# Batch 2's k loads later, each batch's second k turn earlier, and one pair of score groups in other PSUM banks

## The chip, the cores and the metric

The kernel runs on one core of a Trainium2 chip. The metric is the device time of one execution in microseconds (us). Three timed runs of the kernel before gave 306.77, 304.9 and 306.38, median 306.38 us; lower is better. The profile is of one more execution.

## The reference

For each of 8 batches and 8 heads of width 64, 576 queries attend to the last 64 positions (a causal sliding window); the result, as 4608 rows of 512 values, goes through two matrix products with a gate between.

```
scores = q @ k.T / sqrt(64)                    # 8 batches, 8 heads, 576 x 576
mask   = (i - j >= 0) & (i - j < 64)
attn   = softmax(where(mask, scores, -1e9))
x      = attn @ v  -> rows (batch, position), columns (head, d): 4608 x 512
h      = x @ w_in                              # 512 -> 2048
out    = (h * cos(h)) @ w_out                  # 2048 -> 512, float32
```

Inputs and outputs are float32; the kernel multiplies in bf16.

## The kernel before, in words

**Two streams.** The second part (the products with w_in and w_out) goes through the 4608 rows in nine tiles of 512 rows. For a tile, PE (TensorE) forms 16 blocks of h (L443), ScalarE takes a sine of each (L589), VectorE multiplies (L592), and PE multiplies by w_out (L604, 64 matmuls for a tile). The attention of a batch is cut into units of 64 queries by 128 keys (two heads of a pair, one query block), and units into groups of three or four. While tile t is in its second product, batch t + 1 goes through its softmax, group by group:

- scores on PE into a PSUM bank (`blocks_64`, L305), several groups by one call of `g_scores_across`;
- on VectorE the mask and the row maximum, one instruction a unit (`g_max`, L329); when it has run, the bank is free;
- the exponential on ScalarE, one a unit (`g_exp`, L340), its reciprocal sum on VectorE (`g_inv`, L347);
- the normalized weights w (`g_norm`, L354), for nearly all groups on GpSimd (POOL), for batch 1's first three on VectorE;
- the turn of w: for the groups in DIRECT by PE into a slot of the pool `ps_t` (`tw_ps`, L363) and a copy by VectorE (`g_put`, L117); for the others by a DMA transpose on SyncE's queue (`wT`, L366);
- the values on PE (`values`, L381), which read v, and the cast of their result (`put_x`, L117).

**Banks.** PSUM has eight. Five have names (O0, O1, X0, X1, S); a tile of the same name waits until the last one was read. The other three are the slots of `ps_t`, given out in turn: to the transposes `tw_ps`, the values `o_ps`, and in later batches to some scores. Batch 1's groups, counted from 0 here, get their scores in pairs: 0 and 1 in X1 and S, 2 and 3 in X0 and X1, 4 and 5 in S and X0, 6 and 7 in X1 and S, 8 and 9 in X0 and X1, 10 and 11 in S and X0. Groups 0 to 5, 8 and 9 of batch 1 are turned by PE, 6, 7, 10 and 11 by DMA.

**q, k and v.** From batch 2 on, q and k are loaded in five chunks each by GpSimd's DMA queue (`load_chunk`, L165), with the cast to bf16, and turned by a DMA transpose on SyncE's queue (`turn`, L250): q by one, k by two, the first for chunks 0 and 1, the second for chunks 2 to 4. The first part of a batch's scores reads the first turn of k, the second part both. v is loaded by GpSimd's queue (`load_v`, L171); its half blocks are copied to other partitions, for batch 1 by two DMAs on SyncE's queue (`spread_v`, L180), later by VectorE.

**What sets the order.** The program writes each engine's order itself. `at(time, step)` puts a step in a plan, `pump(time)` emits the steps that are due, and the main loop calls it between matmuls; the times are in steps of the plan, 32 to a tile, and not in us. Nothing is reordered after that: an instruction that waits holds up all behind it on its engine, and a DMA that waits holds up all behind it on its queue. Two kinds of rows keep q, k and v of two batches, so that loads for batch b + 1 run beside batch b.

Of the kernel before, what the change touches and what calls it, by code (L numbers as in the profile page):

```python
# [40 lines left out]
T = 2 * Q  # L41
# [23 lines left out]
def kernel(  # L65
# [44 lines left out]
    S_BANKS = ("X1", "S", "X0")  # L110
# [356 lines left out]
    def at(time, fn, *args):  # L467
        plan.append((time, len(plan), fn, args))
# [9 lines left out]
    n = n_first  # L478
    for t in range(B - 1):
        last = max(i for i, units in enumerate(groups) if units[0][0] == t + 1)  # L480
        time = T * t + Q - 1.4
        for i in range(last + 1 - n):
            time += PACE * len(groups[n - 1]) if i else 0
            if t and i == 4:
                time = max(time, T * t + Q + 4.3)
            if t == 0 and i % 2 == 0:
                at(time, g_scores_across, n, 2, (S_BANKS + S_BANKS)[i % 3:])
            elif t and i in (0, 4):
                at(time, g_scores_across, n, last + 1 - n if i else 4, "t t t S X1 X0".split() if i else "t t t X1".split())
            lags = LAGS[:2] + tuple(T * t + T - 0.65 - time + 0.01 * s for s in range(3)) if n == last and t else LAGS  # L490
            if t == 0 and i in (8, 9):
                lags = LAGS[:2] + ((2.2, 2.25) if i == 8 else (2, 2.05)) + LAGS[-1:]
            for lag, fn in zip(lags, (g_max, g_exp, g_inv, g_norm)):
                at(time + lag, fn, n, *("d" for _ in range(1) if fn is g_norm and n < n_first + 3))
            lag = (6.3 if t else 5.5 if i == 3 else 4.6) if n in direct else lags[-1]
            at(time + lag, g_trans, n)
            if n in direct:
                at(time + lag + 0.3, g_put, n)
            ready.update({unit: time + (lag + 1.3 if n in direct else 8.5) for unit in groups[n]})
            n += 1  # L500

    for b in range(1, B):
        t0 = T * (b - 1)
        if b > 1:
            for i, name in enumerate(("q", "k")):
                for c in range(NC):
                    time = 4 + 0.5 * (c + NC * i) if b == 2 else t0 - T + 8 + 0.9 * (c + NC * i)
                    if i and c > (3 if b == 2 else 1):
                        time = 26.9 if b == 2 else t0 - T + 22.5 + 1.5 * (c - 2)
                    at(time, load_chunk, name, b, c)  # L510
                for c, (lo, hi) in enumerate(((0, 2), (2, NC)) if i else ((0, NC),)):
                    at(t0 + 2.5 if c else t0 - (5.8 if b > 2 else 3.4) + 0.1 * i, turn, name, b, lo, hi)
            for c in range(5):
                at(t0 + 3.5 + 0.9 * c, load_v, b, c)
            for time, part in ((13.5, 0), (19.9, 2), (21.7, 3)):
                at(t0 + time, spread_v, b, part, None)
# [5 lines left out]
    for mt in range(1, n_mt):  # L522
        for p in range(PAIRS):
            time = max(ready[b, p - p % 2 + i // TU, j] for i in range(2 * TU) for b, j in (divmod(mt * TU + i % TU, NU),))
            time = max(time, 25.5) if mt == 1 else T * mt - (8.01 if mt == n_mt - 1 else 1.01)
# [118 lines left out]
```

## Time and profile before

| | before |
|---|---|
| timed runs, us | 306.77, 304.9, 306.38 |
| median, us | 306.38 |
| the profiled execution's own time, us | 305.0 |
| its span, us | 302.9 |
| PE busy, us | 286.5 |
| VectorE (DVE), ScalarE (ACT), GpSimd (POOL) busy, us | 221.4, 235.0, 172.2 |
| GpSimd's DMA queue (q0), SyncE's (q1), share of 16 DMA engines | 79.3%, 47.3% |
| HBM read and written, MB | 36.70, 9.44 |

The span goes from the first to the last instruction of the program; 2.1 us of the execution's own time lie around it. A row of the timeline is: start in us, length in us, engine, line, operation, output<-input, shape, count, and in brackets how long the engine had been idle and what ended that. SPq is SyncE's queue; its length is that of issuing, not of the transfer. A row of stretches is: from:to, length, then busy us and count of PE, PEld (weight loads), DVE, ACT, POOL, the granted clock, the share of the 16 DMA engines (several packets of one may overlap, so it can pass 1) and GB/s. A row of waits is: who <- for whom: us in all, times, the longest. A row of DMA issues is: output<-input, queue, count, KB each, us from issue to landing. A row of a DMA queue is: packets, MB, share of the engines. A row of the chain is: start, us, what. A row of one tile's instructions is: line, engine, operation, count, then the shortest, median and longest in ns, and the first and last start in us.

### The profile page before, as it was taken

To read this page: it belongs to the slowest core of one execution; us is meant where nothing else is said; L and a number is where in the kernel's file an instruction comes from. 1 tells how busy PE (TensorE), PEld (TensorE's weight loads), DVE (VectorE), ACT (ScalarE), POOL (GpSimd) and SP (SyncE) were. 2 spreads that over 40 slices of the span, in tenths; PEclk is the share of its full clock that TensorE was granted. 3 is DMA by queue.
4 is the path that set the end of the run, shared out by engine and by line. 5 is a ranking of instruction groups with operands and counts; after the bars stand their busy time and mean duration, and the time that the engine had idled before them with its cause. 6 is when DMAs were issued, how large, how long until landed. Compare 5 with 4: busy or idle time off the path is not lost.

```text
span 302.9 us, 8058 instructions
## 1 busy us (share of the span) xinstructions
PE 286.5 (95%) x2726; PEld 148.4 (49%) x2762; DVE 221.4 (73%) x852; ACT 235.0 (78%) x783; POOL 172.2 (57%) x204
## 2 busy tenths in 40 slices
PE   3789997999999999999999999989999999999996
PEld 2568743544454445444544454444544454454443
DVE  3899897778967897789678967896789778236701
ACT  5897898678997799879987998799869996116600
POOL 8997369792799368945995599549803620000000
PEclk9999999999999999999999999999999999999999
DMA  8999999999999999999999999999993470012011
GB/s 171 172 197 210 207 163 164 115 145 142 220 164 144 177 181 173 131 184 195 93 159 151 232 154 162 141 220 161 171 198 119 89 176 16 3 69 72 0 69 69
DMA packets 164841, 43.75 MB, mean 144 GB/s; under 512 B 153920, under 2 KB 160064, under 8 KB 164800
## 3 DMA queue, kind: packets, MB, share of 16 engines
q0 software_dynamic: 99360, 18.06, 79.3%
q1 hardware_dynamic: 65296, 24.98, 47.3%
q8 instruction: 21, 0.34, 0.5%
q14 instruction: 20, 0.16, 0.2%
q10 hardware_dynamic: 144, 0.20, 0.2%
HBM read 36.70 MB, written 9.44 MB: 152 GB/s over the span
## 4 chain that ended last, share of the span: by engine, by line
PE 67%; DMA 15%; POOL 6%; DVE 6%; issue 4%; ACT 0%; SPq 0%; POOLq 0%; DVEq 0%
PE h_ps L443 31%; PE out_ps L604 28%; DMA v<-in_v_dram 5%; DMA kX<-k 4%; POOL w L354 4%; DMA k<-in_k_dram 3%; DMA v<-v 3%; PE o_ps L381 2%; DVE s L329 2%; PE s_ps L305 2%; PE out_ps L455 1%; POOL v L171 1%; DMA q<-in_q_dram 1%; DVE negm L325 1%; PE tw_ps L363 1%
## 5 line engine op out<-in xcount | busy, mean ns | idle before, releaser
L604 PE MATMUL out_ps<-w_out,gT 128*128 128x512 bf16 x542 | 124.0, 379 | 1.7 <-issue 1.3
L443 PE MATMUL h_ps<-xT,w_in 128*128 128x512 bf16 x497 | 111.0, 379 | 1.1 <-issue 0.2
L354 POOL TENSOR_TENSOR w<-e,rden 128x512 bf16<-128x512 f32 (+1 forms) x75 | 73.0, 984 | 59.9 <-DVE rden L347 56.3
L592 DVE TENSOR_TENSOR gT<-h_ps,sin 128x512 bf16<-128x512 f32 x128 | 84.9, 688 | 30.2 <-ACT sin L589 30.2
L340 ACT ACTIVATE e<-s,negm 128x128 f32<-128x128 f32 x256 | 99.2, 403 | 1.9 <-DVE negm L329 1.8
L589 ACT ACTIVATE sin<-h_ps 128x512 f32<-128x512 f32 x128 | 73.7, 599 | 28.6 <-PE h_ps L443 28.1
L604 PEld LDWEIGHTS <-gT 128*128 128x128 bf16 x560 | 52.7, 98 | 60.5 <-issue 0.4
L443 PEld LDWEIGHTS <-w_in 128*128 128x128 bf16 x512 | 49.9, 98 | 59.1
L329 DVE CUSTOM_DVE_ANT_0 s<-s_ps,mask 128x128 f32<-128x128 f32 x256 | 57.9, 283 | 1.9 <-PE s_ps L305 1.7
L340 ACT ACTIVATION_READ_ACCUMULATOR e<-s,negm 128x1 f32 x256 | 51.9, 203 | 0.0
L171 POOL DMA_DIRECT2D v<-in_v_dram x40 | 34.1, 870 | 6.6 <-DMA w_out<-in_moe_w_out_dram 4.2
L117 ACT COPY out_sb<-out_ps 128x512 f32<-128x512 f32 (+1 forms) x18 | 10.5, 582 | 24.9 <-PE out_ps L604 19.3
L165 POOL DMA_DIRECT2D k<-in_k_dram x30 | 26.4, 893 | 1.7 <-DMA v<-in_v_dram 1.6
L165 POOL DMA_DIRECT2D q<-in_q_dram x30 | 25.4, 886 | 3.1 <-DMA w_out<-in_moe_w_out_dram 3.1
L117 DVE CAST xT<-o_ps 128x512 bf16<-128x512 f32 x28 | 18.3, 679 | 9.6 <-PE o_ps L381 9.3
L117 DVE COPY out_sb<-out_ps 128x512 f32<-128x512 f32 x18 | 12.3, 681 | 14.9 <-PE out_ps L604 14.9
L329 DVE DVE_READ_ACCUMULATOR2_ANT negm<- 128x1 f32 x256 | 20.9, 82 | 0.0
L347 DVE RECIPROCAL rden<-den 128x4 f32<-128x4 f32 (+1 forms) x80 | 13.5, 171 | 9.6 <-ACT e L340 7.7
L420 PE MATMUL h_ps<-xT,w_in 128*128 128x256 bf16 x128 | 15.5, 273 | 0.0
L420 PEld LDWEIGHTS <-w_in 128*128 128x128 bf16 x128 | 12.0, 98 | 1.4
L117 DVE COPY v<-v 64x1024 bf16<-64x1024 bf16 (+1 forms) x19 | 11.4, 601 | 0.4
L426 ACT ACTIVATE sin<-h_ps 128x512 f32<-128x512 f32 x16 | 9.1, 597 | 2.9 <-PE h_ps L420 2.9
(60 smaller groups left out, 187.5 us busy)
## 6 DMA issues: line engine op xcount, KB each, us to landing
out_dram<-out_sb SPq DMA_DIRECT2D x16, 512.0 KB, 7.7
v<-in_v_dram POOLq DMA_DIRECT2D x32, 128.0 KB, 6.2
q<-in_q_dram POOLq DMA_DIRECT2D x24, 128.0 KB, 8.7
k<-in_k_dram POOLq DMA_DIRECT2D x24, 128.0 KB, 7.9
w_in<-in_moe_w_in_dram POOLq DMA_DIRECT2D x2, 768.0 KB, 11.1
w_out<-in_moe_w_out_dram POOLq DMA_DIRECT2D x1, 1024.0 KB, 12.9
w_out<-in_moe_w_out_dram POOLq DMA_DIRECT2D x2, 512.0 KB, 15.5
wT<-w SPq DMA_TRANSPOSE x58, 5.0
```

The source lines that it names most:

```text
L117: {"a": nc.scalar.copy, "p": nc.gpsimd.tensor_copy}.get(engine, nc.vector.tensor_copy)(out, in_)
L165: nc.gpsimd.dma_start(out=st[name, b][:n, c].rearrange("p (h d) -> p h d", h=H), in_=src.rearrange("h p d -> p h d"))
L171: nc.gpsimd.dma_start(out=vt.rearrange("p (h d) -> p h d", h=H), in_=v[b, :, c * 128:c * 128 + n, :].rearrange("h p d -> p h d"))
L329: nc.vector.tensor_tensor_reduce(out=s[:, u], in0=s_ps[:, u], in1=mask[:, 2 - j % 2 if j else 0], scale=-scale if b else -1.0, scalar=BIG, ...
L340: nc.scalar.activation(e[:, u], s[:, u], AF.Exp, bias=negm[:, u:u + 1], scale=1.0 if n < n_first else -1.0, accum_out=den[:, u:u + 1])
L347: nc.vector.reciprocal(out=rden[:, 0:len(groups[n])], in_=den[:, 0:len(groups[n])])
L354: (nc.gpsimd if engine == "p" else nc.vector).tensor_tensor(out=w[:, 0:u], in0=e[:, 0:u], op=ALU.mult, in1=rden[:, 0:u].unsqueeze(2).to_br ...
L420: nc.tensor.matmul(out=st["h0", i][:, e], lhsT=w_in_sb[:, ks, ff * 128:ff * 128 + 128], rhs=st["xT", 0][:, ks, half], start=ks + e == 0, s ...
L443: nc.tensor.matmul(out=st["h", ff], lhsT=w_in_sb[:, ks, ff * 128:ff * 128 + 128], rhs=st["xT", mt][:, ks], start=start, stop=stop)
L589: nc.scalar.activation(sin, h_ps, AF.Sin, bias=math.pi / 2.0)
L592: nc.vector.tensor_tensor(out=gt[:, e], in0=h_ps, in1=sin, op=ALU.mult)
L604: nc.tensor.matmul(out=o_ps[e], lhsT=gT[ff // 2][:, ff % 2, ms * 128:ms * 128 + 128], rhs=w_out_sb[:, ff], start=ff == 0, stop=ff == n_ff - 1)
```

## The change

Three edits, all to the plan; every instruction of before is still there, once.

1. Batch 1's groups 8 and 9: scores in bank X0 and in the next slot of `ps_t`, where they had X0 and X1.
2. Batch 2's five k loads: at 27.1 to 27.5 of the plan. Before, four of them were at 6.5 to 8.0 and the last at 26.9. In GpSimd's order the four go from ahead of the w of group 3 to behind the w of group 9, the fifth from ahead of the w of group 9 to behind it, ahead of the w of groups 10 and 11. The order of the DMAs among themselves stays. Other batches' loads stay.
3. The second turn of k, for batches 2 to 7: right behind the first. In SyncE's order it moves ahead of two turns of w for batch 2, of four for batches 3, 4 and 6, and of three for batches 5 and 7 (there one turn of w stays between the two of k). Before, it was behind those and ahead of the stores of the tile.

The orders of PE, VectorE and ScalarE are the same, but for the bank.

```diff
             if t == 0 and i % 2 == 0:
-                at(time, g_scores_across, n, 2, (S_BANKS + S_BANKS)[i % 3:])
+                at(time, g_scores_across, n, 2, ("X0", "t") if i == 8 else (S_BANKS + S_BANKS)[i % 3:])
...
             for i, name in enumerate(("q", "k")):
                 for c in range(NC):
                     time = 4 + 0.5 * (c + NC * i) if b == 2 else t0 - T + 8 + 0.9 * (c + NC * i)
-                    if i and c > (3 if b == 2 else 1):
-                        time = 26.9 if b == 2 else t0 - T + 22.5 + 1.5 * (c - 2)
+                    if i and (b == 2 or c > 1):
+                        time = 27.1 + 0.1 * c if b == 2 else t0 - T + 22.5 + 1.5 * (c - 2)
                     at(time, load_chunk, name, b, c)
                 for c, (lo, hi) in enumerate(((0, 2), (2, NC)) if i else ((0, NC),)):
-                    at(t0 + 2.5 if c else t0 - (5.8 if b > 2 else 3.4) + 0.1 * i, turn, name, b, lo, hi)
+                    at(t0 - (5.8 if b > 2 else 3.4) + 0.1 * i + 0.1 * c, turn, name, b, lo, hi)
```

## The prediction

> **What bounds the kernel now.** I read the page first: one line for the span, one for TensorE.
>
> ```profile
> span 302.9 us, 8058 instructions
> PE 286.5 (95%) x2726; PEld 148.4 (49%) x2762; DVE 221.4 (73%) x852; ACT 235.0 (78%) x783; POOL 172.2 (57%) x204
> ```
>
> TensorE is the bound; all its idle time is 302.9 - 286.5 = 16.4 us. A change that takes no matmul away can win only idle time of PE in the stages that it touches, so next I read the busy time by stage and the list of PE's waits.
>
> ```profile
> 40.00:54.00 14.00, 11.93 (x146) 6.00 (x142) 11.51 (x76) 12.53 (x63) 11.86 (x15) 1.00 2.25 158
> ```
>
> ```profile
> PE tw_ps L363 <- POOL w L354: 1.5, 3, 0.9
> PE s_ps L305 <- DMA kX<-k: 0.6, 1, 0.6
> PE o_ps L381 <- DMA v<-v: 0.4, 1, 0.4
> ```
>
> From 40 to 54 us, while batch 1's softmax runs beside tile 0's second product, PE (the first pair of the row) loses 14.0 - 11.9 = 2.1 us. The first and the third of the waits shown lie there: transposes waiting for GpSimd's normalized weights w, and tile 1's first values waiting for the copy of v. The second, for a turned k, lies at 202 us. These are what the change can win: at most 2.1 + 0.6 = 2.7 us. The timeline of that stage, PE and then POOL:
>
> ```profile
> 46.73 0.24 PE L305 MATMUL s_ps<-kT,qT 64*64 64x128 bf16 x2
> 47.16 0.36 PE L305 MATMUL s_ps<-kT,qT 64*64 64x128 bf16 x10 [0.18 <-DVE negm L329]
> 47.44 1.04 PE L604 MATMUL out_ps<-w_out,gT 128*128 128x512 bf16 x4
> 49.34 0.34 PE L363 MATMUL tw_ps<-ident,w 128*128 128x128 bf16 x3 [0.86 <-POOL w L354]
> 50.12 0.34 PE L363 MATMUL tw_ps<-ident,w 128*128 128x128 bf16 x3 [0.45 <-POOL w L354]
> 50.30 1.03 PE L604 MATMUL out_ps<-w_out,gT 128*128 128x512 bf16 x3
> 51.16 0.33 PE L363 MATMUL tw_ps<-ident,w 128*128 128x128 bf16 x3
> ...
> 52.63 0.28 PE L381 MATMUL o_ps<-wT,v 128*64 128x64 bf16 x6
> 53.36 0.60 PE L381 MATMUL o_ps<-wT,v 128*64 128x64 bf16 x26 [0.44 <-DMA v<-v]
> 54.12 1.67 PE L604 MATMUL out_ps<-w_out,gT 128*128 128x512 bf16 x7 [0.16 <-issue]
> ```
>
> ```profile
> 44.86 3.54 POOL L165 DMA_DIRECT2D k<-in_k_dram  x4
> 48.46 2.39 POOL L354 TENSOR_TENSOR w<-e,rden 128x384 bf16<-128x384 f32 x3
> ...
> 54.67 0.83 POOL L354 TENSOR_TENSOR w<-e,rden 128x384 bf16<-128x384 f32 x1 [0.20 <-DVE rden L347]
> ```
>
> POOL issues batch 2's k loads for 3.54 us, and the three w behind them (groups 3, 4, 5) start with no wait of their own at 48.46: they were ready, and stood in line. PE stands still for the first two. The row at 54.67 is group 9's w. On VectorE:
>
> ```profile
> 46.32 0.17 DVE L347 RECIPROCAL rden<-den 128x3 f32<-128x3 f32 x1
> ...
> 47.28 0.17 DVE L347 RECIPROCAL rden<-den 128x3 f32<-128x3 f32 x1
> ...
> 48.46 0.29 DVE L329 CUSTOM_DVE_ANT_0 s<-s_ps,mask 128x128 f32<-128x128 f32 x1
> ...
> 50.50 0.36 DVE L117 COPY wT<-tw_ps 128x384 bf16<-128x384 bf16 x1 [0.43 <-PE tw_ps L363]
> 50.77 0.17 DVE L347 RECIPROCAL rden<-den 128x3 f32<-128x3 f32 x1
> ...
> 51.25 0.29 DVE L329 CUSTOM_DVE_ANT_0 s<-s_ps,mask 128x128 f32<-128x128 f32 x1
> ```
>
> The two first rows are groups 3's and 4's reciprocals, 48.46 is the last piece of group 8's maximum, 50.50 the copy of group 4's transposed weights, 50.77 group 6's reciprocal, and 51.25 the last piece of group 9's maximum. VectorE keeps that order in the changed kernel.
>
> **The change, part by part.**
>
> *Batch 2's k loads behind group 9's w.* POOL is free at 44.9 instead of 48.4. Group 3's w then starts when its reciprocal is done, 46.32 + 0.17 = 46.5, and takes 2.39 / 3 = 0.80: ready at 47.3. Group 4's: 47.28 + 0.17 = 47.45, ready at 48.3.
>
> *Group 9's scores in a slot of the transposes.* Groups 8 and 9 take twelve matmuls, of which the third waits for bank X1, which VectorE is still reading for group 6 (the released row at 47.16). From start to start the pair takes 47.44 - 46.73 = 0.71, its last ten 47.44 - 47.16 = 0.28, so without the wait some 0.28 x 12 / 10 = 0.34: 0.37 is won, since group 9's slot was last used three transposes ago. It has a price: the three slots go round, and now group 5's transposes get the slot of group 9's scores (before, that of group 2's transposes). They wait until VectorE has taken group 9's maximum, which stands in its queue behind the copies of groups 3 and 4 and group 6's reciprocal.
>
> The walk on PE: output product at 47.07; four matmuls (51.16 - 50.30 = 0.86) to group 3's transposes at 47.9, w is there; group 4's at 48.36 (0.06 after its w, as now: 48.46 + 2 x 0.80 = 50.06 and 50.12); 51.16 - 50.12 = 1.04 to group 5's, which PE reaches at 49.4. VectorE ends group 8's maximum at 48.46 + 0.29 = 48.75, the copy of group 3 takes 50.77 - 50.50 = 0.27, and from the copy of group 4 to the end of group 9's maximum it is 51.25 + 0.29 - 50.50 = 1.04: 50.06. Group 5's transposes start at 50.15, after a new wait of 0.75, yet 1.0 before their present 51.16. From there to the values it is 52.63 - 51.16 = 1.47: 51.62 instead of 52.63. If v's copy has landed, 0.1 for the first six and 54.12 - 53.36 = 0.76 for the rest bring the output product to 52.48 instead of 54.12: **1.65 us won.** With bank X1 kept, group 4's w at 48.3 sets the pace all the same, group 5's transposes would start at 49.5 and the values at 51.0; so the slot costs 0.6 here.
>
> *Does v's copy land in time?* It must land by 51.6; now it lands just before 53.36, where PE's wait ends.
>
> ```profile
> v<-v SPq DMA_DIRECT2D x1, 256.0 KB, 7.8
> q<-in_q_dram POOLq DMA_DIRECT2D x1, 64.0 KB, 5.8
> q0 software_dynamic: 2547, 0.32, 130.0%
> q1 hardware_dynamic: 442, 0.43, 53.4%
> q1 hardware_dynamic: 1678, 0.43, 114.0%
> ```
>
> The rows of q0 and the first of q1 are the stretch 46.6 to 50.6: GpSimd's queue (the last q and the k loads) moved 2,547 small packets while SyncE's moved the 0.43 MB of v's copy, in 4 us. The last row is 58 to 60: SyncE's queue alone moved 0.43 MB in 2 us. The last q load, issued some 0.7 before k's first at 44.86, lands 5.8 later at 50.0; with k gone nothing of POOL's queue comes after it. The bounds for the copy's landing are thus about 50.0 and, if k's packets never mattered, 53.3. I take the early end: that both queues moved at once, and that one alone is twice as fast, says that k's packets cost the copy time. [...]
>
> *k comes later: who waits?* Five loads of k, four of which were out by 48.4, now go behind group 9's w. That one ends at 54.67 + 0.83 = 55.5 now; its reciprocal stands on VectorE behind the first values, which come some 1.0 earlier or more, so I take 54.5. Five issues of 3.54 / 4 = 0.89 follow, to 58.9, ahead of the w of groups 10 and 11 and the v and q loads, which all come up to 2 us later.
>
> ```profile
> k<-in_k_dram POOLq DMA_DIRECT2D x1, 128.0 KB, 8.6
> k<-in_k_dram POOLq DMA_DIRECT2D x1, 64.0 KB, 4.0
> q<-in_q_dram POOLq DMA_DIRECT2D x2, 128.0 KB, 11.5
> kX<-k SPq DMA_TRANSPOSE x1, 6.6
> kX<-k SPq DMA_TRANSPOSE x1, 11.8
> 72.33 0.64 PE L305 MATMUL s_ps<-kX,qX 64*64 64x128 bf16 x32
> 78.19 0.75 PE L305 MATMUL s_ps<-kX,qX 64*64 64x128 bf16 x40
> ```
>
> A k load takes 4.0 us in light traffic and 8.6 in the present heavy one; batch 2's two turns took 6.6 and 11.8. First turn: its second chunk is issued at 55.4, so it lands between 55.4 + 4.0 + 6.6 = 66.0 and 55.4 + 8.6 + 6.6 = 70.6, and is wanted at 72.33 - 1.65 = 70.7. Second turn: last chunk issued at 58.0, landing between 58.0 + 4.0 + 6.6 = 68.6 and 58.0 + 8.6 + 11.8 = 78.4, wanted at 78.19 - 1.65 = 76.5. I take no wait: v and q loads that made the present one slow now come after it. The weights' turns of groups 10 and 11 stand behind both on SyncE, up to 11.8 us later than now, and are wanted by tile 2's values, which PE reaches only after the whole of the second product that these scores interrupt.
>
> *The second turn right behind the first, batches 3 to 7.* SyncE's weights' turns (one to four a batch) go behind it.
>
> ```profile
> 190.57 11.46 DMA kX<-k
> 211.66 1.04 PE o_ps L381 x59
> ```
>
> Batch 6's second turn is issued at 190.57 behind four weights' turns, lands at 202.03, and PE waits 0.6. Moved ahead of them it is issued some 6 us earlier: **0.6 us won.** The four go behind it, by about 5 us; the values that read them start at 211.66, and they have 8 us or more. The other batches' second turns do not hold PE now and come earlier; costed at nothing.
>
> *Sum:* 1.65 + 0.6 = 2.25. The profiled execution took 305.0, its span 302.9; the timed ones run from 304.9 to 306.77 with median 306.38. I set the sum against the middle of profiled run and median, 305.7: **303.4 us**.
>
> **The rivals.**
>
> *v's copy is no earlier.* Then the values start at 53.36 as now and all that was won before is given back there; only the 0.6 stays: 305.1. For it: no row shows the copy alone. Against it: the rates above.
>
> *The slot costs nothing.* If VectorE reaches group 9's maximum early enough, the 0.75 is not waited: 303.4 - 0.6 = 302.7, bounded by the copy's landing at 51.0. Against it: the order on VectorE is fixed and has copies of groups 3 and 4 ahead.
>
> *Slower: batch 2's second turn is late.* Its scores want it at 76.5, and every us past that is a us of PE: at the upper bound of 78.4 it costs 1.9, which leaves 305.3, and from 76.5 + 2.25 = 78.8 on the kernel is slower than before. If the last chunk of k took the 11.5 us that two q loads took at 64 to 66 us, the turn would land at 58.0 + 11.5 + 11.8 = 81.3, and the time would be 303.4 + 4.8 = 308.2. For it: k now travels beside q's turn and moves towards that heavy stretch. Against it: even with a turn of 11.8 us the last chunk may take 6.7 us, and the later traffic that made it 11.8 (v and q for the next batches) now comes behind it.
>
> Whether the issues themselves come late, now that they stand beside VectorE's copies and casts, this row bears on:
>
> ```profile
> L165 POOL DMA_DIRECT2D k<-in_k_dram x30: 733/939/974, 44.9 to 209.5; - x30
> ```
>
> Over all 30 issues the longest took 0.97 against a median of 0.94, beside a VectorE that is busy 73%: no issue here was held up. [...] By the row I give that no more than 0.05 of the chance below.
>
> **How the numbers follow.** Forecast (2.25 won, give or take half a us) 0.56; copy no earlier 0.20; slot free 0.10; second turn late 0.14, of which 0.07 ends slower than before. The likeliest case alone spans 302.4 to 304.6, since single runs differ by up to 1.9. The range of 301.8 to 306.2 takes in the first three and the mild part of the fourth. A measurement of this kernel can tell about 1%, 3 us, from no change; the forecast is 0.75%, so most of it counts as the same: faster by over 1% 0.18 (the free slot and the lucky half of the forecast), within 1% 0.75, slower 0.07.
>
> **What would show it.** PE's waits for GpSimd's w fall from 1.5 to about half of it; a new wait of about 0.75 appears at a transpose near 50 us, released by VectorE's maximum; the wait for v's copy is gone, and the copy's 7.8 us become 6 or less; the first s_ps from kX starts near 70.7; PE's wait for kX is gone. Wrong would be: the values again released by the copy at 53, a wait for kX at 71 or 77, or stage 40 to 54 as long as before with the wait merely under another name.

## The result and the profile after

| | before | after |
|---|---|---|
| median of the timed runs, us | 306.38 (5 runs, 304.9 to 307.09) | 302.33 (5 runs, 302.15 to 303.44) |
| ratio after / before, 95% interval | | 0.9899 [0.9866, 0.9932] |
| the profiled execution's own time, us | 305.0 | 302.33 |
| its span, us | 302.9 | 300.6 |
| outside the span, us | 2.1 | 1.7 |

The forecast was 303.4 in a range of 301.8 to 306.2, most likely within 1% of before; it came out 1.0% faster. The interval lies on both sides of that 1%, so the measurement doesn't tell "within 1%" (given 0.75) from "faster by over 1%" (given 0.18). The profiled executions differ by 2.67 us, the medians by 4.05. Both differences have to be explained, and they are not the same thing.

The page of the kernel after, its first lines:

```profile
span 300.6 us, 8056 instructions
PE 285.7 (95%) x2726; PEld 147.8 (49%) x2762; DVE 221.8 (74%) x852; ACT 234.4 (78%) x783; POOL 171.9 (57%) x204
```

PE's idle time is 300.6 - 285.7 = 14.9 us, after 16.4. The stretch from 40 to 54 us (the first pair is PE's busy time and count):

```profile
40.00:54.00 14.00, 12.95 (x147) 6.63 (x149) 13.06 (x85) 13.38 (x68) 9.14 (x12) 1.00 1.48 124
```

PE loses 14.0 - 12.95 = 1.05 us there instead of 2.1. Two of its waits after, from the list of PE's waits; the one for kX is no longer in it:

```profile
PE o_ps L381 <- DMA v<-v: 0.5, 1, 0.5
PE tw_ps L363 <- POOL w L354: 0.4, 2, 0.2
```

The timeline of that stage, PE and then GpSimd:

```profile
46.57 0.36 PE L305 MATMUL s_ps<-kT,qT 64*64 64x128 bf16 x12
46.87 1.04 PE L604 MATMUL out_ps<-w_out,gT 128*128 128x512 bf16 x4
47.74 0.33 PE L363 MATMUL tw_ps<-ident,w 128*128 128x128 bf16 x3
48.31 0.34 PE L363 MATMUL tw_ps<-ident,w 128*128 128x128 bf16 x3 [0.24 <-POOL w L354]
...
49.36 0.33 PE L363 MATMUL tw_ps<-ident,w 128*128 128x128 bf16 x3
...
51.66 0.60 PE L381 MATMUL o_ps<-wT,v 128*64 128x64 bf16 x26 [0.55 <-DMA v<-v]
52.41 1.67 PE L604 MATMUL out_ps<-w_out,gT 128*128 128x512 bf16 x7 [0.16 <-issue]
```

```profile
46.51 2.54 POOL L354 TENSOR_TENSOR w<-e,rden 128x384 bf16<-128x384 f32 x3 [1.20 <-DVE negm L329]
...
53.77 4.26 POOL L165 DMA_DIRECT2D k<-in_k_dram  x5
```

The reader sees three things. GpSimd's w of groups 3 to 5 start at 46.51 instead of 48.46, now after an idle time of GpSimd's own (1.20), and PE's two long waits for them are down to 0.24 and one shorter still. Group 5's transposes start at 49.36 with no wait in brackets. The values wait for v's copy, 0.55 where it had been 0.44, but end so that the output product starts at 52.41 instead of 54.12: 1.71 us. Of these, 0.16 were there ahead of all that the change touches (the transposes before group 3's, at 43.10 against 43.26), so that the stage itself wins some 1.55. That is more than the 1.05 by which PE's idle time there falls, because a wait in brackets begins at the end of the matmul before it: four output matmuls are 1.04 long, and where nothing is waited for the next row starts 0.87 after theirs (46.87 and 47.74). Each wait costs up to some 0.17 more than its brackets say.

Further on, SyncE's turns of k and the scores that read them:

```profile
62.53 4.90 SPq L250 DMA_TRANSPOSE kX<-k  x2
```

```profile
70.62 0.64 PE L305 MATMUL s_ps<-kX,qX 64*64 64x128 bf16 x32
76.48 0.75 PE L305 MATMUL s_ps<-kX,qX 64*64 64x128 bf16 x40
```

Batch 6's second scores, before and after:

```profile
202.16 0.75 PE L305 MATMUL s_ps<-kX,qX 64*64 64x128 bf16 x40 [0.62 <-DMA kX<-k]
```

```profile
199.77 0.78 PE L305 MATMUL s_ps<-kX,qX 64*64 64x128 bf16 x40
```

None of the three scores of after has a wait in brackets. Batch 2's two turns, one right behind the other, are issued at 62.53 and 65.03, take 6.1 and 8.3 us and land at 68.64 and 73.33, 2.0 and 3.2 us before they are wanted. From the end of batch 6's first scores to the end of its second it is 6.0 us now and was 6.7.

So the profiled executions give 1.71 near 50 us, 0.6 at batch 6, and some 0.35 outside the span: 2.67 in all. The rest of the difference of the medians, 1.4 us, is in none of the lines above. The experiments had to find it.

### The profile page after: what moved, and what is told of

Read it like the earlier page. It is cut to its first block, busy times and chain, and to the rows that moved or that the text cites. A ratio compares the mean times of both kernels' runs of the same rounds, so it can differ in the third digit from the quotient of the medians.

```text
span 300.6 us, 8056 instructions
## 1 busy us (share of the span) xinstructions
PE 285.7 (95%) x2726; PEld 147.8 (49%) x2762; DVE 221.8 (74%) x852; ACT 234.4 (78%) x783; POOL 171.9 (57%) x204
## 4 chain that ended last, share of the span: by engine, by line
PE 78%; DMA 13%; POOL 3%; DVE 2%; issue 2%; SPq 0%; POOLq 0%
PE h_ps L443 36%; PE out_ps L604 35%; DMA v<-in_v_dram 8%; DMA k<-in_k_dram 3%; PE s_ps L305 2%; PE o_ps L381 2%; DMA v<-v 2%; PE out_ps L455 1%; DVE xT L117 1%; POOL w L354 1%; PE tw_ps L363 1%; DVE s L329 1%; POOL v L171 1%; POOL k L144 1%; POOL w_in L196 0%
## 5 line engine op out<-in xcount | busy, mean ns | idle before, releaser
L340 ACT ACTIVATION_READ_ACCUMULATOR e<-s,negm 128x1 f32 x256 | 48.1, 188 | 0.0
L117 DVE COPY out_sb<-out_ps 128x512 f32<-128x512 f32 x18 | 12.2, 680 | 14.9 <-PE out_ps L604 14.9
L347 DVE RECIPROCAL rden<-den 128x4 f32<-128x4 f32 (+1 forms) x80 | 13.6, 171 | 10.6 <-ACT e L340 7.4
```

The costliest lines, as they stand in the source:

```text
L117: {"a": nc.scalar.copy, "p": nc.gpsimd.tensor_copy}.get(engine, nc.vector.tensor_copy)(out, in_)
L340: nc.scalar.activation(e[:, u], s[:, u], AF.Exp, bias=negm[:, u:u + 1], scale=1.0 if n < n_first else -1.0, accum_out=den[:, u:u + 1])
L347: nc.vector.reciprocal(out=rden[:, 0:len(groups[n])], in_=den[:, 0:len(groups[n])])
```

## Experiments

Each was timed in five rounds beside the kernel before on the same chip. The executions of one kernel fell into two heaps, told apart by the mean granted clock of the execution: 0.998 to 1.0, or 0.993 to 0.994 (once 0.989). Below, "at full clock" is the mean over the executions of the first heap. By their scatter, a difference of two such means is known to 0.4 to 0.8 us (95%). Means of one series, on one chip, are compared where there are such. For the five runs of before in the table of the result no clock is on record.

| kernel | median, us | ratio to before, 95% interval | at full clock, us | low clock |
|---|---|---|---|---|
| before, beside e1 to e4 | 305.4 | | 304.71 | 13 of 29 |
| before, beside e5 to e8 | 305.89 | | 304.92 | 12 of 19 |
| before, beside e9, e10 | 305.82 | | 304.94 | 9 of 17 |
| before, beside e11, e12 | 305.74 | | 305.06 | 8 of 16 |
| after, first series | 302.33 | 0.9899 [0.9866, 0.9932] | 302.67 | 0 of 5 |
| e1, loads and turns, old bank | 302.87 | 0.993 [0.9905, 0.9956] | 302.85 | 0 of 6 |
| e2, loads alone | 304.63 | 0.9981 [0.9961, 1.0001] | 304.38 | 2 of 12 |
| e3, turns alone | 304.83 | 0.999 [0.9966, 1.0013] | 304.42 | 4 of 12 |
| e4, bank alone | 305.56 | 1.0012 [0.9988, 1.0036] | 304.68 | 8 of 12 |
| e5, before with small k loads | 303.52 | 0.9929 [0.9902, 0.9957] | 303.52 | 0 of 8 |
| e6, before with two w on VectorE | 305.61 | 0.9981 [0.9955, 1.0007] | 305.14 | 3 of 12 |
| e7, after with later values | 302.26 | 0.9891 [0.9864, 0.9919] | 302.45 | 0 of 6 |
| e8, e7 with the old bank | 302.71 | 0.9898 [0.9869, 0.9927] | 302.68 | 0 of 6 |
| e9, before with PE kept at work | 306.4 | 1.003 [1.0004, 1.0055] | 306.43 | 1 of 12 |
| e10, e7 with batch 3's k behind w | 301.62 | 0.9868 [0.9834, 0.9903] | 301.89 | 0 of 6 |
| e11, after again | 302.9 | 0.9909 [0.9881, 0.9938] | 302.76 | 1 of 12 |
| e12, e10 again | 301.86 | 0.9882 [0.985, 0.9915] | 301.97 | 0 of 5 |

### e1: the loads and the turns, without the bank

The change without its first edit (groups 8 and 9 stay in X0 and X1).

```diff
-                at(time, g_scores_across, n, 2, ("X0", "t") if i == 8 else (S_BANKS + S_BANKS)[i % 3:])
+                at(time, g_scores_across, n, 2, (S_BANKS + S_BANKS)[i % 3:])
```

> Edits 2 and 3 without edit 1: groups 8 and 9 keep banks X0 and X1. Theory (v's copy sets the start of the values, so what the bank wins ahead of it is waited away): PE reaches the values some 0.4 us later than in the changed kernel, waits some 0.4 us less for v's copy, and the values' main part starts at the same 51.7 us give or take 0.3; span within 0.3 us of the changed kernel's 300.6. Rival (the bank carries part of the gain by itself): span 301.0 or more, and the values' main part starts at 52.1 or later. The prediction's own step, that the slot costs 0.6, would give a span of 300.0.

At full clock 302.85 against 302.67 and 302.76 for the whole change. PE, in the profile of e1:

```profile
47.23 0.35 PE L305 MATMUL s_ps<-kT,qT 64*64 64x128 bf16 x10 [0.17 <-DVE negm L329]
...
51.92 0.60 PE L381 MATMUL o_ps<-wT,v 128*64 128x64 bf16 x26 [0.57 <-DMA v<-v]
```

The wait for bank X1 is back, 0.17, but v's copy ends the stage all the same. The bank's 0.1 to 0.2 us, between different series, can't be told from nothing.

### e2: the loads alone

```diff
-                    if i and c > (3 if b == 2 else 1):
-                        time = 26.9 if b == 2 else t0 - T + 22.5 + 1.5 * (c - 2)
+                    if i and (b == 2 or c > 1):
+                        time = 27.1 + 0.1 * c if b == 2 else t0 - T + 22.5 + 1.5 * (c - 2)
```

> Edit 2 alone: batch 2's k loads behind group 9's w; banks and turns as before. Theory: the stage from 40 to 54 us wins its 1.7 us in full (values' main part at 51.7 instead of 53.4), PE's waits for w fall from 1.5 to under 0.5, and the wait of 0.6 for the turned k of batch 6 stays; span 301.2. Rival (the turns have to move with the loads): the second turn of batch 2, issued behind two turns of w as before but with k landing later, is late for the scores at 76.5 us, PE waits there, and the span is 302 to 304.

Only 0.33 us is won at full clock, give or take 0.5. PE in the profile of e2, and between the rows of PE that of SyncE's queue for batch 2's second turn:

```profile
53.31 0.60 PE L381 MATMUL o_ps<-wT,v 128*64 128x64 bf16 x26 [1.66 <-DMA v<-v]
```

```profile
69.05 3.99 SPq L250 DMA_TRANSPOSE kX<-k  x1
```

```profile
79.14 0.75 PE L305 MATMUL s_ps<-kX,qX 64*64 64x128 bf16 x40 [0.93 <-DMA kX<-k]
```

Left behind two turns of w, batch 2's second turn is issued at 69.05, not at 62.5 to 65, lands at 79.0, and PE waits 0.93. In this one execution v's own loads were late too (the copies are issued at 46.99, in before at 44.70), and PE stood 1.66 us for the copy; whether others have that is not seen. The wait at 79 is the rival of the late second turn, in the kernel without the third edit: the later loads need the earlier turn.

### e3: the turns alone

```diff
-                    at(t0 + 2.5 if c else t0 - (5.8 if b > 2 else 3.4) + 0.1 * i, turn, name, b, lo, hi)
+                    at(t0 - (5.8 if b > 2 else 3.4) + 0.1 * i + 0.1 * c, turn, name, b, lo, hi)
```

> Edit 3 alone: the second turn of k right behind the first; loads and banks as before. Theory: nothing changes before 60 us, PE's wait of 0.6 us for the turned k of batch 6 goes, span 302.3 (0.6 below 302.9). Rival (the turns carry more than half of the gain, through less traffic at other places): span 301.5 or less.

0.29 us at full clock, give or take 0.5. PE's two waits for w are as before:

```profile
49.63 0.34 PE L363 MATMUL tw_ps<-ident,w 128*128 128x128 bf16 x3 [1.32 <-POOL w L354]
...
50.42 0.34 PE L363 MATMUL tw_ps<-ident,w 128*128 128x128 bf16 x3 [0.44 <-POOL w L354]
```

The time outside the span is 1.78 us here against 2.12 of before, which alone makes 0.34. The wait for kX is gone from its profile, but the mean span at full clock is 302.6 in both kernels: the theory's 0.6 is not in it. Loads alone win 0.33, turns alone 0.29, both (e1) 1.86: 1.2 more than the sum of 0.62, give or take 0.8. Neither alone can be told from nothing; together they pay.

### e4: the bank alone

```diff
-                at(time, g_scores_across, n, 2, (S_BANKS + S_BANKS)[i % 3:])
+                at(time, g_scores_across, n, 2, ("X0", "t") if i == 8 else (S_BANKS + S_BANKS)[i % 3:])
```

> Edit 1 alone: group 9's scores in a slot of the transposes; loads and turns as before. Theory: PE wins the 0.2 to 0.4 us of the wait for bank X1 and waits them away again at the transposes of group 3, whose w is held up on POOL behind the k loads until 49.3 us; span 302.9 within 0.3. Rival (the bank is worth its 0.4 us): span 302.5. The prediction's step of a new wait for the slot would show as an idle stretch ahead of group 5's transposes, released by VectorE's maximum.

No gain: 304.68 at full clock against 304.71. But the profiled execution of e4 is one of those with the low clock, and so it shows where the clock goes. The clock by 40 slices, from the page; then two stretches (the clock is the last but two); then PE and GpSimd:

```profile
PEclk9999998899999999999999999999999999999999
```

```profile
48.00:51.50 3.50, 0.86 (x9) 0.39 (x8) 1.34 (x12) 3.12 (x17) 3.44 (x5) 1.00 1.68 192
51.50:55.00 3.50, 3.28 (x13) 1.28 (x11) 1.55 (x11) 1.26 (x6) 2.04 (x3) 0.51 1.89 136
```

```profile
50.50 0.34 PE L363 MATMUL tw_ps<-ident,w 128*128 128x128 bf16 x3 [2.20 <-POOL w L354]
51.28 0.34 PE L363 MATMUL tw_ps<-ident,w 128*128 128x128 bf16 x3 [0.44 <-DVE wT L117]
```

```profile
39.68 0.88 POOL L165 DMA_DIRECT2D q<-in_q_dram  x1 [0.88 <-DMA w_out<-in_moe_w_out_dram]
...
46.02 3.54 POOL L165 DMA_DIRECT2D k<-in_k_dram  x4
49.62 2.39 POOL L354 TENSOR_TENSOR w<-e,rden 128x384 bf16<-128x384 f32 x3
```

In this execution the first of q's loads, released by a transfer of w_out, is issued at 39.68, in the profiled one of before at 38.54. So k's loads go out at 46.02 instead of 44.86 and w starts at 49.62 instead of 48.46, 1.16 later; PE is not later, and its wait for w is 2.20 us and not 0.86. PE works 0.86 us of the 3.5 from 48.0 to 51.5. Right after it the granted clock is a half, for 3.41 us (51.54 to 54.95, worked out from finer stretches: its mean is 0.70 from 51.50 to 51.60 and 0.74 from 54.90 to 55.00; by stretches of 1 us from 51 to 55 it is 0.77, 0.50, 0.50 and 0.52), and then full again. A half less for 3.41 of 304.5 us makes a mean of 0.994, which is that of the low heap; where the low clock lay in the other executions no trace shows. Executions of before with the low clock are 306.06 - 304.71 = 1.35 us longer than the others (in the three later series 1.57, 1.37 and 1.41). That the wait of PE brings the clock down is a theory at this point; e9 tries it.

### e5: before, with k's loads made small

Batch 2's first four k loads bring 16 of their 128 rows, so its scores are not those of the reference.

```diff
-        n = min(128, S - 128 * c)
+        n = 16 if (name, b) == ("k", 2) and c < 4 else min(128, S - 128 * c)
```

> The kernel before, but batch 2's first four k loads take only 16 of each head's 128 rows: their issues still hold up POOL, their packets are nearly gone. It leaves out most of that load. Theory (two costs: issues hold up w, packets hold up v's copy): the waits for w stay (1.3 to 2 us at groups 3 and 4), v's copy lands 1 to 2 us earlier than 53.2, PE no longer waits for it, and about 0.5 us is won at the values. Rival (k's packets never mattered to v's copy): the copy lands at 53 as before and PE's wait of 0.4 stays.

303.52 at full clock, 1.40 less than before, and no low clock in 8. GpSimd, PE, and v's copy in the list of DMA issues:

```profile
44.85 2.13 POOL L165 DMA_DIRECT2D k<-in_k_dram  x4
```

```profile
48.30 0.75 PE L363 MATMUL tw_ps<-ident,w 128*128 128x128 bf16 x6
...
52.09 0.60 PE L381 MATMUL o_ps<-wT,v 128*64 128x64 bf16 x26 [0.57 <-DMA v<-v]
```

```profile
v<-v SPq DMA_DIRECT2D x1, 256.0 KB, 6.3
```

Two effects that the run was meant to part came together: four small loads hold GpSimd for 2.13 us and not 3.54, so w is in time and both waits are gone, and v's copy takes 6.3 us and not 7.8. The part of each can't be told from this run, and the waits for w did not stay, against what was expected. What it shows is that k's loads in these 8 us are what costs, since the order, the banks and the turns are all those of before.

### e6: before, with two of the w on VectorE

```diff
-                at(time + lag, fn, n, *("d" for _ in range(1) if fn is g_norm and n < n_first + 3))
+                at(time + lag, fn, n, *("d" for _ in range(1) if fn is g_norm and n < n_first + 5))
```

> The kernel before, with the w of groups 3 and 4 made by VectorE: PE no longer waits for POOL there, while the k loads and their packets stay where they were. Theory: in executions at full clock PE reaches the values earlier and waits it away for v's copy, which lands at 53 as before: no gain over the kernel before at full clock (304.7). The half-clock stretch near 51.5 us, which a long wait for w brought in the run with the bank alone, comes in fewer executions than the kernel before's 13 of 29: at most 2 of 12. Rival (the half clock has nothing to do with the wait for w): 4 to 7 of 12.

The waits for w are gone and nothing is won: 305.14 at full clock against 304.92. PE:

```profile
49.40 0.35 PE L305 MATMUL s_ps<-kT,qT 64*64 64x128 bf16 x10 [0.87 <-DVE negm L329]
...
55.18 0.60 PE L381 MATMUL o_ps<-wT,v 128*64 128x64 bf16 x26 [1.34 <-DMA v<-v]
```

With VectorE laden with two w (0.56 us each), the wait turns up at bank X1 (0.87), and the copy of v, with k's packets still beside it, ends the stage as before (1.34; v's loads were late in this execution, its copies issued at 46.70). Made on VectorE, an early w does not pay. That k's packets must be gone from the copy as well is not shown by this run alone, since VectorE's own delay came in; the times of the copy below bear it out. The low clock is rarer, 3 of 12, but not gone: between the 2 of the theory and the 4 of the rival.

### e7 and e8: the values later

The changed kernel with tile 1's first values four output matmuls later, so that the copy has landed; e8 the same with the old bank.

```diff
-            time = max(time, 25.5) if mt == 1 else T * mt - (8.01 if mt == n_mt - 1 else 1.01)
+            time = max(time, 27.05) if mt == 1 else T * mt - (8.01 if mt == n_mt - 1 else 1.01)
```

> The changed kernel, with tile 1's first two values emitted four output matmuls later (plan time 27.05 instead of 25.5 at the least). Theory (v's copy, at 51.5, is the last of the three waits): PE does 0.87 us of other work in the 0.55 us that it waited, so the wait is gone and the span is 0.4 to 0.6 below the changed kernel's: 300.1. Rival (VectorE's queue, in which the cast of the first values now stands later, takes it back): span 300.6 or more.

> The same with groups 8 and 9 in X0 and X1 as before (without edit 1). Theory: with v's copy out of the way, what the bank wins is no longer waited away, so this one is 0.3 to 0.4 us slower than with edit 1. Rival (the bank gives nothing even then): the same within 0.2 us.

302.45 and 302.68 at full clock, against 302.67: no gain that can be told, nor a difference between the two, though the wait for v is gone from both profiles. In e7 PE is 0.4 us ahead at batch 2's second scores (76.02 against 76.48), and loses it here, PE and then GpSimd:

```profile
82.57 0.40 PE L363 MATMUL tw_ps<-ident,w 128*128 128x128 bf16 x4 [0.52 <-POOL w L354]
```

```profile
79.53 1.04 POOL L354 TENSOR_TENSOR w<-e,rden 128x512 bf16<-128x512 f32 x1 [0.24 <-DVE rden L347]
80.51 0.94 POOL L165 DMA_DIRECT2D k<-in_k_dram  x1
81.47 1.05 POOL L354 TENSOR_TENSOR w<-e,rden 128x512 bf16<-128x512 f32 x1
```

The w that PE waits for starts right behind a k load of 0.94 with no idle time of its own: it is the case of batch 2's loads again, one batch on.

### e9: PE kept at work during the wait

The kernel before, with 24 transposes of the identity ahead of group 3's, into the slot that group 3 then overwrites.

```diff
             st["tw", n] = t_ps = ps_t.tile([128, GF, 128], BF16, tag="t", name="tw_ps")
+            if n == n_first + 3:
+                for _ in range(24):
+                    nc.tensor.transpose(t_ps[:, 0], ident, ident)
```

> The kernel before, with 24 extra transposes of the identity by PE (into the slot that group 3's transposes then overwrite) right ahead of group 3's transposes: PE works during the first wait for w instead of standing still; four such matmuls take 0.23 us from start to start, so 24 take some 1.4, against a wait of 0.86 in the profiled execution of the kernel before and 2.20 in that of the run with the bank alone. The order of everything else and GpSimd's late w stay. Theory that standing still for w is what halves TensorE's clock: executions with a mean clock below 0.997 fall from about half (13 of 29, 12 of 19) to at most 1 in 10; the median falls to 304.7 to 305.1, since group 4's transposes wait for w until 50.1 anyway and the extra matmuls cost 0.0 to 0.5 in an execution at full clock. Rival that the low clock belongs to something else that the moved loads change (the DMA traffic, the late values): about half of the executions stay low and the median stays at 305.4 to 306.

The low clock falls from 9 of 17 to 1 of 12 in the same series. GpSimd's w are as late as before (from 48.59, in before from 48.46); only PE's standing still is gone:

```profile
48.52 1.50 PE L364 MATMUL tw_ps<-ident 128*128 128x128 bf16 x24
49.85 0.74 PE L366 MATMUL tw_ps<-ident,w 128*128 128x128 bf16 x6
```

That bears out the theory of the clock, and the other kernels fit: where the transposes wait long for w (before, e3, e4) 54 of 105 executions are low, where w is in time (e1, e2, e5 to e8, e10 to e12, after) 6 of 78. What lowers the clock in these six is not known. The time of e9 does not fit: 306.43 at full clock, 1.5 above before, where 0.0 to 0.5 was expected. The stage itself costs nothing (the output product starts at 53.97, before at 54.12). What is lost shows up 100 us on, where second turns of k are late: PE waits 1.8 us for kX in two places, where before waits 0.62 in one; of the two, one is

```profile
172.01 0.81 PE L305 MATMUL s_ps<-kX,qX 64*64 64x128 bf16 x44 [0.74 <-DMA kX<-k]
```

Why these turns come later here (batch 5's is issued at 161.00 instead of 160.13) is open. It does show how near to the edge they stand in the kernel before.

### e10, e11, e12: batch 3's k behind the w, and the changed kernel beside it

e10 and e12 are e7 with batch 3's last three k loads moved behind the two w; e11 is the changed kernel.

```diff
-                        time = 27.1 + 0.1 * c if b == 2 else t0 - T + 22.5 + 1.5 * (c - 2)
+                        time = 27.1 + 0.1 * c if b == 2 else t0 - T + (25.2 + 0.2 * (c - 2) if b == 3 else 22.5 + 1.5 * (c - 2))
```

> The changed kernel with tile 1's first values four output matmuls later (as in the run with the values later), and batch 3's third, fourth and fifth k loads behind the w of the groups that PE transposes near 82.6 and 84.6 us, where two stood between those w. Theory that the gain of the later values is given back because GpSimd's w, which PE's transposes wait for at 82.6, stand behind a k load of 0.94: that wait (0.5) goes, the values of batch 2 end at 87.3 instead of 87.8, the span is 300.2 instead of 300.6, the time 301.8 to 302.2 (0.4 less than both). Rival that the give-back lies elsewhere (VectorE's maximum or ScalarE's exponential set the pace of those w): the wait stays and the time stays at 302.3 to 302.7. If batch 3's second turn of k then lands after 107.6, where its scores want it, the time is up to 1 longer.

> The changed kernel unaltered, beside the next run on the same chip, so that the two can be compared. Theory that the low clock belongs to the long wait for w: no execution below a clock of 0.997, time 302.3 to 302.8. Rival that its five executions at full clock were luck: one execution in three or more is low.

> The changed kernel with the later values and batch 3's k loads behind the two w, again. If its 0.8 over the changed kernel is real, its mean is 0.5 to 0.9 below that of the changed kernel in this call; if it was chance or the chip, the two agree within 0.3. In a profiled execution whose start is not late, the values of batch 2 should end at 87.3 and the span be 300.2.

At full clock e10 gives 301.89, and in one series e12 gives 301.97 and e11 302.76: 0.79 less, give or take 0.6, as much as between e10 and the first series. PE in the profile of e12:

```profile
82.84 0.39 PE L363 MATMUL tw_ps<-ident,w 128*128 128x128 bf16 x4
```

The wait is gone, and from the end of batch 2's second scores to the end of its values it is 10.3 us, where the changed kernel has 10.6 (11.3 in e11) and e7 11.2. The single profiles of e10 and e12 began late (batch 2's second scores are at 77.63 and 76.97, in after at 76.48) and have spans of 301.4 and 300.7, so the 300.2 that was expected of them is not seen there; the mean spans at full clock are 300.1 and 300.2. This version is faster than both kernels, and e7's gain was indeed given back behind a k load. The changed kernel has one low clock in 12 in e11, with 306.04 us; together with the kernels that keep its loads and turns it is 1 of 46.

## Why the prediction was right, and where it was not

**Loads off GpSimd's way: right, to a tenth.** Group 3's w was put at 46.5 and started at 46.51. Group 4's transposes were put at 48.36 and started at 48.31 (0.16 of lead in that profile, as said above). PE's waits for w went from 1.5 to 0.4, further down than to the half that was named. The five k issues, now beside VectorE's casts, took 4.26 us, 0.85 each, the longest 0.94, where the longest of before was 0.97: none was held up.

**The slot of group 9: wrong.** The step said that the three slots go round, so that group 5's transposes get that of group 9's scores and wait 0.75 for VectorE. They do not go round here. The bank of each slot's use, in the order of the program, around groups 3 to 5 (s9 is group 9's scores, tw3 to tw5 the transposes, o the first values):

```
before:          tw3 in 7   tw4 in 5   tw5 in 6   o in 7   o in 5
after:  s9 in 7  tw3 in 5   tw4 in 6   tw5 in 5   o in 6   o in 7
```

Group 5 got bank 5, which group 3's copy had left, and not bank 7, whose reader (group 9's maximum) stands behind that copy in VectorE's order: the slot that came free first in the order of the program. It started at 49.36 with no wait, where 50.15 was forecast. The rival of the free slot had this outcome, but by another reason (VectorE early). In e4, with the same bank, group 5's transposes have no wait in brackets either (53.08).

**v's copy: the mechanism right, the landing 1.5 late.** The step took the early one of its bounds, 50.0; the copy landed at 51.52, after 5.72 us instead of 7.8, between the bounds. So a wait of 0.55 for the copy stands in place of the 0.75 at the slot, and the values went on at 51.66 where 51.62 was forecast: two errors, of 0.75 and 0.55, with opposite signs. That the 1.65 of this stage came out as 1.71 (1.55 without the lead of 0.16) is in good part luck. What the step had wrong is that the copy is through when the last of GpSimd's queue is. Two stretches of 2 us, each from 2.5 to 4.5 us after the first issue of v's copy, GpSimd's queue and SyncE's, first before (47.20 to 49.20), then after (47.62 to 49.62), and the copy after:

```profile
q0 software_dynamic: 1067, 0.13, 110.2%
q1 hardware_dynamic: 277, 0.27, 62.4%
```

```profile
q0 software_dynamic: 361, 0.04, 46.1%
q1 hardware_dynamic: 325, 0.31, 78.0%
```

```profile
v<-v SPq DMA_DIRECT2D x1, 256.0 KB, 5.7
```

With a third of GpSimd's packets beside it the copy moves 0.31 MB and not 0.27: faster, but far from twice as fast. The row of 58 to 60 that the step took its factor of two from is of turns, in packets of 0.26 KB and not 1 KB, and bears little on a copy. (The stretch of the prediction, 46.6 to 50.6, can't show the rate: it holds nearly all of the copy's 0.46 MB in both kernels, 0.43 and 0.44.)

The other profiles show the size. The larger of the two copies takes 7.0 to 7.8 us in the five kernels with k's full loads beside it (before, e3, e4, e6, e9), 5.4 to 5.9 in six with these moved (after, e1, e2, e7, e11, e12), and 6.3 in e5, where only k's loads are smaller. None comes near the 4.6 that a landing at 50.0 makes of the issue at 45.39 of before.

**Batch 2's turns: right.** First landing 66.0 to 70.6, measured 68.64; second 68.6 to 78.4, measured 73.33; the scores wanted them at 70.7 and 76.5, and started at 70.62 and 76.48. The rival that ends slower needs the second turn late; e2, with the loads moved and the turn left, has such a wait in its profile, and 1.5 of the 1.86 us are missing in its time.

**Batch 6: the wait gone, its price not shown.** 0.6 was named, and the wait of 0.62 is gone from the profile of after. But it was sized from one execution. Of the kernels without the third edit, the second scores start 6.4 to 7.0 us after the first in the profiles of before, e5 and e9, and 5.9 after them in those of e2, e4 and e6, as in after. And e3, which has the third edit alone, shows no gain within its mean span. The term belongs to some executions, and a mean over many wins less than 0.6.

**The sum.** 2.25 was forecast, 2.67 measured between the profiled executions: 2.3 in the span and some 0.35 outside it. Between the means at full clock of one series (before and e11) it is 2.30: 1.96 in the span, 0.34 outside. The part outside is 1.75 to 1.79 us for all kernels with the third edit, 2.11 to 2.13 for those without, but 1.78 for e6, which has none of the edits. By the pages, at 2726 records of PE, the kernels with the short time have 8056 instructions or fewer (8053 in e6) and those with the long one 8058; no run tries whether that is the cause. No step of the prediction had this term, and it made up for some 0.3 that the span fell short of the 2.25.

**The base.** The text set 2.25 against 305.7, a middle of 305.0 and 306.38, and took the difference for scatter. There is a term of its own in it: 42 of 81 executions of before have a low mean clock, at 1.35 to 1.57 us each, and of 46 with the moved loads and turns one has it. At full clock before takes 304.7, and 304.7 - 2.25 = 302.45 is within 0.2 us of what was measured (median 302.33, mean 302.67). So the forecast of 303.4 is 1.1 too high by its base, which the range took in; that the sum fits so well on the right base owes something to the term outside the span. The first series' median of 306.38 is a low-clock value by its size: three of its five runs, the median among them, lie above 305.79, the longest of 39 executions of before at full clock in the later series. Of the 4.05 by which the medians differ, 2.0 is won at full clock (304.7 to 302.7), some 1.4 is the low clock, and the rest is the scatter of two medians of five. Side by side with more runs (before and e11) the medians are 305.74 and 302.9, 2.8 apart.

Why only half of the executions of before have the low clock is not shown. The wait is 0.86 us in the profile of before, at full clock, and 2.20 in that of e4, which has the half clock; in the 3.5 us ahead of the drop in e4 PE worked 0.86.

## What to carry to other kernels

Here a DMA issue on GpSimd, a computing engine, cost the w behind it 0.9 us a load, and its packets cost the transfer beside it (v's copy took 7.0 to 7.8 us with k's loads beside it, 5.4 to 5.9 with these moved); loads that are wanted much later belong behind the work that is wanted now, together with what consumes them, since moving the loads without their turns won 0.33 us, which can't be told from nothing, and both 1.86. When the runs of one kernel scatter by 1.4 us in two heaps, look at the mean clock of each before setting a base: in e4 a wait of 2.20 us at TensorE was followed by 3.41 us of half clock, and the low executions of before are 1.35 to 1.57 us longer. A wait seen in one profile may belong to that execution alone; compare several before it goes into a sum. Where a pool hands out slots, read the banks from the built program and do not assume a rotation.

## What the hardware showed that was not expected

In e4 TensorE's granted clock fell to 0.5 for 3.41 us in the midst of a kernel whose PE is 95% busy, after a stretch of 3.5 us with 0.86 of work. Filling the wait with 24 transposes of the identity brought the low mean clock from 9 of 17 executions to 1 of 12 (e9). A k load of 16 rows held GpSimd for 2.13 / 4 = 0.53 us (e5), one of 128 rows for 0.89: the larger issue took 0.36 more. A copy of 256 KB on SyncE's queue took 7.0 to 7.8 us beside GpSimd's small packets of k and 5.4 to 5.9 without them.
